# Chunk 0's joins by 64-row products of block-diagonal operands, and sums of squares ahead of the second pair of turned keys, in a delta-rule attention with a feed-forward behind it

## The chip, the cores and the metric

The kernel runs on one core of one Trainium2 chip. The metric is the device time in microseconds; less is better. A run of the unchanged kernel gives a median of 650.97 us over three (650.86 to 651.51). Besides that there is one profiled execution, from which all durations are taken.

## The reference

Four batches and eight heads of 768 tokens with 48 features go through a delta-rule recurrence; the result, as 3072 rows of 384, goes through a feed-forward with SiLU.

```python
    k_n = k / (np.linalg.norm(k, axis=-1, keepdims=True) + 1e-06)
    for t in range(S):
        kt, vt, bt = (k_n[:, :, t], v[:, :, t], beta[:, :, t, None])
        y[:, :, t] = np.einsum('bhd,bhde->bhe', q[:, :, t], state)
        v_old = np.einsum('bhde,bhd->bhe', state, kt)
        state = state + bt[:, :, :, None] * np.einsum('bhd,bhe->bhde', kt, vt - v_old)
...
    h = x @ w_in
    g = h * (1.0 / (1.0 + np.exp(-h)))
    return (g @ w_out).astype(np.float32)
```

`w_in` is 384 x 2048, `w_out` 2048 x 384, everything in 32-bit floats.

## The kernel before

**Tiling.** The sequence is cut into six chunks of 128 tokens, a chunk into two halves (`hf`) of 64, a half into two blocks of T = 32. The four batches form two groups `g` of two; a group has 16 heads (HH). A chunk's recurrence becomes a triangular system in the scores of the keys with each other. Its diagonal 32x32 blocks are inverted for all heads at once, with the (block, head) pairs on the 128 partitions, on VectorE (`invert_first` for chunk 0, `invert` for the others); TensorE then joins the inverted blocks to 64x64 inverses (`xi`), by which the values are multiplied (`inner`, L830). Chunk 0 is made in two halves, so that its feed-forward can start early: `joins(0)` runs before anything of the feed-forward, `joins(1)` in pieces between its products.

**Chunk 0's inversion and joins.** `invert_first` inverts only the 16x16 corners of each 32x32 block (`x`), for both corners at a time: one multiplication by `step` (L658), 15 pairs of L666 and L670, one last multiplication (L673). Q = 16 is the size of a corner. Two transposes bring the result from pairs on partitions to tokens on partitions: `low` (L680, the first 16 rows of each block) and `up` (L684, all of it). POOL copies the second half of the identity into `y` (L681). Then come the stages that `joins` (L1364) lists:

- `corner(g, hf)`: the scores of a 32-row block, transposed, by `low`: one product of 32x32 by 32x16 for each of two blocks of 16 heads (L707). Two operations on VectorE (L714, 64 rows each) multiply by the mask `second`, add the identity `pick`, and write `y`.
- `turned(g, hf)`: `up` by `y` for the even block of each head (L723), copied out to `xes` by ScalarE and VectorE.
- `straight(g, hf)`: `y` by `up` for both blocks, two products of 32x32 by 32x32 for each head (L736), copied out in four pieces to the diagonal blocks of `xi`.
- `merge_half(g, hf, second)`: two stages of 16 products of 32x32 (L796) for the off-diagonal block.

All is in 32-bit floats, for which each product stands twice in TensorE's program: 16 products are 32 pairs of a weight load (PEld) and a matmul (PE) in the profile. So a `corner` or `straight` is 64 pairs, a `turned` or a `merge_half` 32, and one `joins` 128 + 64 + 128 + 128 = 448.

`joins` takes a list `between`, one entry behind each stage: `sizes_0` finishes the key lengths on VectorE (L420, L423), `sized` multiplies half of the values by them on POOL (`size_half`, L447, which waits for the operation of VectorE named last), and `filled(n)` and `begin_next` run steps of `narrow`.

**Front.** Keys of chunk 0 are loaded in four batches by six transfers; POOL squares them (`square`, L375), TensorE transposes them (`turn`, L490), VectorE or ScalarE copies them out (L502, L504), TensorE makes the key-by-key blocks (`first_blocks`, L1274), VectorE sums the squares (`add_squares`, L379) and computes the reciprocal lengths with three Newton steps (`norm_steps`, L393 to L413). `beta_of` (L351, L354) brings the gates to tokens on partitions. `block_steps` (L435, L440) makes `step`; `blocks_in` is the VectorE transpose of the blocks. `busy(n)` (L338) issues n products of 128x128 by 128x384 that nobody reads (two passes each).

**Weights.** `w_in` comes in eight pieces of 768 KB (`fetch_w_in(i)`), `w_out` likewise. `narrow` rewrites a piece by two operations on ScalarE (L226, L227), two on VectorE (L231, L235) and one on POOL (L239), the steps of which are spread by `fill`, `begin_next` and their like.

**What sets the order.** `pin` keeps every engine's instructions in the order of the program text; nothing is reordered. Loads go out from SP in one line (`in_line`). `linked(fetch, ...)` lets the next transfer wait until the one before it in line has landed. While chunk 0's inversion runs, a list of words per step places `first_score` ("s", L519), `turn` of the queries ("u"), `score` with the queries ("w") and `busy` ("b", behind the named step). After `joins(0)` one long text (`script`) orders what follows by hand: "s" a step of chunk 0's solve (`inner`, `first_outputs`, ...), "f" a step of `narrow`, "j5" five pairs of `joins(1)`, "r" a piece of the feed-forward (`hidden`, L1031), "T" and "q" transposes of chunk 1, "W7" `fetch_w_in(7)`.

## Time and profile before

| | |
|---|---|
| time, median of three | 650.97 us |
| profiled execution: its time, its span | 653.34 us, 651.36 us |
| granted TensorE clock, mean | 0.976 |

Busy time in stretches of 10 us:

| us | PE | DVE | ACT | POOL | PE clock | GB/s |
|---|---|---|---|---|---|---|
| 10 to 20 | 6.48 | 8.73 | 1.78 | 3.35 | 0.75 | 196 |
| 20 to 30 | 9.68 | 8.97 | 8.52 | 1.94 | 0.74 | 163 |
| 30 to 40 | 5.29 | 7.01 | 2.95 | 6.90 | 0.60 | 151 |
| 40 to 50 | 6.16 | 3.91 | 4.96 | 1.82 | 0.50 | 170 |
| 50 to 60 | 10.00 | 5.08 | 5.60 | 1.85 | 0.87 | 167 |
| 60 to 70 | 9.85 | 8.04 | 8.24 | 3.75 | 1.00 | 132 |
| 70 to 80 | 9.62 | 8.76 | 7.05 | 8.39 | 1.00 | 182 |

PE, DVE, ACT, POOL and SP are TensorE, VectorE, ScalarE, GpSimd and the engine that issues the loads. "PE clock" is the share of full speed that was granted. In rows of the timeline, "x21" is a count, and "[2.84 <-issue]" says that the engine had been idle for 2.84 us and that no other engine or transfer is seen to have released it. The first product of the feed-forward (L1031) starts at 56.55 us.

### The profile page before, as it was taken

How to read it: one execution, taken by the hardware profiler on the slowest of the kernel's cores; microseconds unless marked ns; L12 is line 12 of the kernel's file. 1: busy time of each engine (PE TensorE's matmuls, PEld its weight loads, DVE VectorE, ACT ScalarE, POOL GpSimd, SP SyncE). 2: the span in 40 equal slices, each digit the busy share in tenths (PEclk: the TensorE clock that was granted, in tenths of full speed). 3: DMA queues.
4: the chain of work that ended last, by engine and by line, in shares of the span. 5: the costliest groups of instructions: out<-in, count | busy, mean ns of one | idle time of the engine just before them, and what ended most of it. 6: DMA issues, size and time to landing. Idle time of an engine off the chain costs nothing.

```text
span 651.4 us, 21809 instructions
## 1 busy us (share of the span) xinstructions
PE 627.3 (96%) x9644; PEld 550.7 (85%) x9644; DVE 394.3 (61%) x902; ACT 216.3 (33%) x505; POOL 95.7 (15%) x96
## 2 busy tenths in 40 slices
PE   6859999999999999999999999999999999899997
PEld 4648778666789988989989989989989989789997
DVE  5955979988764985554975453986455963103112
ACT  1646666251351122451122451122451122351111
POOL 5231730337011020010020010020011000000000
PEclk9758999999999999999999999999999999999999
DMA  9675444160369433269243259334163023100101
GB/s 171 141 185 149 148 123 105 49 146 3 78 129 155 60 77 46 60 131 159 43 94 34 57 126 151 59 77 50 41 140 71 24 68 43 40 13 1 25 0 25
DMA packets 141310, 53.68 MB, mean 82 GB/s; under 512 B 112912, under 2 KB 134672, under 8 KB 141216
## 3 DMA queue, kind: packets, MB, share of 16 engines
q1 hardware_dynamic: 140880, 52.14, 40.1%
q8 instruction: 76, 1.25, 0.8%
q10 hardware_dynamic: 336, 0.15, 0.1%
q14 instruction: 18, 0.15, 0.1%
HBM read 39.62 MB, written 10.49 MB: 77 GB/s over the span
## 4 chain that ended last, share of the span: by engine, by line
PE 85%; DVE 8%; DMA 2%; issue 2%; ACT 1%; SPq 1%; POOL 0%; DVEq 0%; POOLq 0%
PE phid L1031 35%; PE px L1138 15%; PE py L1138 11%; PE po L1066 7%; PE pa L519 3%; PE pz L830 3%; DVE rank L617 2%; PE pu L850 2%; PE ph L818 2%; DVE x L622 2%; PE pyc L909 2%; PE pt L490 1%; PE pyc L896 1%; PE px L772 1%; PE py L772 1%
## 5 line engine op out<-in xcount | busy, mean ns | idle before, releaser
L1031 PE MATMUL phid<-xT,w_in 128*128 128x256 f32 x1152 | 258.4, 382 | 2.0 <-DMA xT<-part 2.0
L1031 PEld LDWEIGHTS phid<-xT,w_in 128*128 128x128 f32 x1152 | 215.9, 190 | 33.4 <-issue 3.5
L1041 ACT ACTIVATE gT<-phid 128x512 f32<-128x512 f32 x88 | 52.6, 598 | 143.6 <-PE phid L1031 140.8
L617 DVE SCALAR_TENSOR_TENSOR rank<-g,step,x 128x31 f32<-128x31 f32 (+15 forms) x124 | 49.8, 401 | 35.6 <-DMA g<-blocks 32.2
L1120 DVE TENSOR_TENSOR sums_of_g<-gT 128x384 f32<-128x384 f32 (+1 forms) x60 | 30.1, 521 | 58.9 <-ACT gT L1041 48.3
L1138 PE MATMUL px<-sums_of_w,sums_of_g 128*128 128x192 f32 x320 | 56.8, 329 | 0.0
L1138 PE MATMUL py<-w_out,sums_of_g 128*128 128x192 f32 x320 | 56.8, 329 | 0.0
L1138 PEld LDWEIGHTS px<-sums_of_w,sums_of_g 128*128 128x128 f32 x320 | 52.2, 190 | 0.5
L1138 PEld LDWEIGHTS py<-w_out,sums_of_g 128*128 128x128 f32 x320 | 52.2, 190 | 0.4
L622 DVE TENSOR_TENSOR x<-x,rank 128x31 f32<-128x31 f32 (+15 forms) x124 | 42.5, 342 | 4.3
L457 POOL TENSOR_TENSOR vf<-vf,n_slot 128x768 f32<-128x768 f32 x10 | 15.3, 1539 | 174.5 <-DMA vf<-in_v_dram 123.4
L478 DVE STREAM_TRANSPOSE kq<-stage 128x512 f32<-128x512 f32 x28 | 28.6, 1114 | 8.1 <-DMA stage<-in_q_dram 7.6
L534 ACT COPY xT<-pyc 48x128 f32<-48x128 f32 (+2 forms) x126 | 32.6, 259 | 1.6
L1138 PE MATMUL px<-sums_of_w,gT 128*128 128x192 f32 x160 | 28.4, 329 | 0.0
L1138 PE MATMUL py<-w_out,gT 128*128 128x192 f32 x160 | 28.4, 329 | 0.0
L1138 PE MATMUL px<-w_out,gT 128*128 128x192 f32 x160 | 28.0, 327 | 0.0
L830 PEld LDWEIGHTS pz<-vf,xi 64*64 64x64 f32 x768 | 25.2, 142 | 3.2 <-issue 2.9
L540 POOL COPY g<-x 64x256 f32<-64x256 f32 x4 | 5.0, 1240 | 151.9 <-DVE x L625 151.9
L1138 PEld LDWEIGHTS px<-w_out,gT 128*128 128x128 f32 x160 | 26.4, 190 | 0.5
L830 PE MATMUL pz<-vf,xi 64*64 64x48 f32 x768 | 26.9, 226 | 0.0
L1138 PEld LDWEIGHTS py<-w_out,gT 128*128 128x128 f32 x160 | 26.1, 190 | 0.3
L1138 PEld LDWEIGHTS px<-sums_of_w,gT 128*128 128x128 f32 x160 | 26.1, 190 | 0.2
(197 smaller groups left out, 833.8 us busy)
## 6 DMA issues: line engine op xcount, KB each, us to landing
vf<-in_v_dram SPq DMA_DIRECT2D x48, 96.0 KB, 3.3
out_dram<-o SPq DMA_DIRECT2D x42, 96.0 KB, 2.2
w_out<-in_moe_w_in_dram SPq DMA_DIRECT2D x4, 768.0 KB, 6.0
sums_of_w<-in_moe_w_out_dram SPq DMA_DIRECT2D x4, 768.0 KB, 4.9
blocks<-ap SPq DMA_DIRECT2D x40, 64.0 KB, 1.9
g<-blocks SPq DMA_DIRECT2D x5, 512.0 KB, 3.7
kb<-in_k_dram SPq DMA_DIRECT2D x12, 192.0 KB, 4.6
kb<-in_k_dram SPq DMA_DIRECT2D x24, 96.0 KB, 4.5
```

The lines of the kernel that those rows point to most:

```text
L457: pin(nc.gpsimd.tensor_tensor(out=vf, in0=vf, in1=of, op=ALU.mult))
L478: pin(nc.vector.transpose(out=kqs[c, b][:, :, j, :].rearrange("p a (i m) -> p a m i", i=T), in_=src.rearrange("p a (m d) -> p a m d", d=D) ...
L519: pin(nc.tensor.matmul(pa[e][half, p * n * W : (p + 1) * n * W], lhsT=kq[rows, p, 0, half], rhs=kq[rows, p, js[0] : js[-1] + 1, half], sta ...
L534: return pin(nc.scalar.copy(to, of))
L617: pin(nc.vector.scalar_tensor_tensor(out=tv, in0=g[:, 0:m, m : m + 1].to_broadcast([P, m, n]), scalar=step[:, m : m + 1], in1=x[:, m : m + ...
L622: yield pin(nc.vector.tensor_tensor(out=x[:, 0:m, m:T], in0=x[:, 0:m, m:T], in1=tv, op=ALU.add))
L830: yield pin(nc.tensor.matmul(pz[rows, n * D : (n + 1) * D], lhsT=xis[g][rows, u * H + 2 * p + e, :], rhs=vfs[c][rows, hf, g * HB + u, p, : ...
L1031: pin(nc.tensor.matmul(ph[:, j * GT : (j + 1) * GT], lhsT=w_in[:, a, (2 * f + j) * P : (2 * f + j + 1) * P], rhs=xTs[c, hf][:, a, :], star ...
L1041: pin(nc.scalar.activation(out=hidden_of(c, hf, f), in_=ph[:], func=ACTF.Silu, scale=-0.5 if in_blocks(c) else 0.5))
L1066: pin(nc.tensor.matmul(pos[i][:, 0:DM], lhsT=hidden_of(0, hf, f // 2)[:, at : at + C], rhs=w_outs[f // HFF][:, f % HFF, :], start=(f == 0) ...
L1120: pin(nc.vector.tensor_tensor(out=sums_of_g[:, k, fs], in0=of[0], in1=of[1], op=op))
L1138: pin(nc.tensor.matmul(to, lhsT=at, rhs=quarter(f, *b) if isinstance(b, tuple) else sums_of_w[b][:, f], start=start and f == 0, stop=f == ...
```

## The change

Operands become block-diagonal, so that the two 32-row products of a head are one of 64 rows.

- `y` is replaced by `wides`: 64x64 for each head, with both blocks on the diagonal and zeros beside them, in three places (a work tile, part of `sum_room`, `crossed`). They are filled from `pick_w`, a constant that POOL makes at the start, by three copies on ScalarE; POOL's copy L681 is gone.
- `low` becomes `lows`, 32 columns for a head: two halves of 16, the second zero for the even block (two POOL memsets behind the inversion), and a copy of the first for the odd one (one copy of 32 rows on ScalarE, one on VectorE, between the two transposes). In the odd blocks the first half holds the same values.
- The lower left 32x32 squares of the key scores are set to zero on POOL (four memsets, behind `first_score`).
- `corner` and `straight` issue 16 products in place of 32. `corner` is followed by four L714 operations of 32 rows in place of two of 64.
- `add_squares` moves ahead of the second pair of `turn`s, whose copies both go to ScalarE; `beta_of(0)` moves between the last two `first_blocks`; `busy(1)` becomes `busy(3)`.
- `load_k(1)` goes ahead of `fetch_w_in(0)`; `load_v(0)` waits for `fetch_w_in(1)`; pieces 5 and 6 of `w_in` change places.
- The words within the inversion, the list `between` and the long text are rewritten.

```diff
+    pick_w = const.tile([P, W], FP32, name="pick_w")
+    pin(nc.gpsimd.memset(pick_w[:], 0.0))
+    for j in range(NB):
+        rows, cols = slice(T * j, T * (j + 1)), slice(T * (j % 2), T * (j % 2 + 1))
+        pin(nc.gpsimd.tensor_copy(out=pick_w[rows, cols], in_=ident[rows, rows]))
...
+    wides = {}
+    def wide_of(n):
+        return wides[n // HH, n % 2][:, n % HH // 2]
...
-        low = sum_room[:, AT_LOW : AT_LOW + BH * Q].rearrange("p (n s) -> p n s", s=Q)
-        y = sum_room[:, AT_G : AT_G + BH * T].rearrange("p (n s) -> p n s", s=T)
...
-        pin(nc.vector.transpose(out=low.rearrange("p n s -> p s n"), in_=x[:, 0:Q, :]))
-        pin(nc.gpsimd.tensor_copy(
-            out=y[:, :, Q:T], in_=pick[:, Q:T].unsqueeze(1).to_broadcast([P, BH, Q])
-        ))
+        lows = sum_room[:, AT_G : AT_G + BH * T].rearrange("p (n i s) -> p n i s", i=2, s=Q)
+        for j in (0, 2):
+            pin(nc.gpsimd.memset(lows[rows[j], :, 1], 0.0))
+        pin(nc.vector.transpose(out=lows[:, :, 0].rearrange("p n s -> p s n"), in_=x[:, 0:Q, :]))
+        for k, by in enumerate((by_act, by_dve)):
+            by(lows[rows[2 * k + 1], :, 1], lows[rows[2 * k + 1], :, 0])
...
-                for j in (2 * k, 2 * k + 1):
-                    cols = slice(T * (j % 2), T * (j % 2 + 1))
-                    pin(nc.tensor.matmul(
-                        pls[k][rows[j], Q * i : Q * (i + 1)], lhsT=aps[0, g][0][rows[j], n % HH // H, n % H, cols],
-                        rhs=low[rows[j], n, :], start=True, stop=True,
+                half = HALVES[k]
+                pin(nc.tensor.matmul(
+                    pls[k][half, T * i : T * (i + 1)], lhsT=aps[0, g][0][half, n % HH // H, n % H, :],
+                    rhs=lows[half, n].rearrange("p i s -> p (i s)"), start=True, stop=True,
+                ))
+                yield
+            for k in range(2):
+                for odd in range(2):
+                    of, at = rows[2 * k + odd], T * odd
+                    pin(nc.vector.scalar_tensor_tensor(
+                        out=wides[g, hf ^ k ^ g][of, :, at : at + Q],
+                        in0=out_of(pls[k], of, T)[:, :, Q * odd : Q * (odd + 1)], scalar=second[of],
+                        in1=pick[of, 0:Q].unsqueeze(1).to_broadcast([T, HH // 2, Q]), op0=ALU.mult, op1=ALU.add,
                     ))
...
-                for j in (2 * k + 1, 2 * k):
-                    pin(nc.tensor.matmul(
-                        pls[k][rows[j], T * i : T * (i + 1)], lhsT=y[rows[j], n, :],
-                        rhs=up[rows[j], n, :], start=True, stop=True,
-                    ))
-                    yield
+                half = HALVES[k]
+                pin(nc.tensor.matmul(
+                    pls[k][half, T * i : T * (i + 1)], lhsT=wide_of(n)[half],
+                    rhs=up[half, n, :], start=True, stop=True,
+                ))
+                yield
...
+    for b in range(B):
+        add_squares(0, b)
     for b in range(2):
         first_blocks(b)
     for b in range(2, B):
-        turn(0, b, 0, (A, CC)[b % 2], b % 2 == 0)
-    for b in range(2, B):
-        first_blocks(b)
-    for b in range(B):
-        add_squares(0, b)
+        turn(0, b, 0, (A, CC)[b % 2], False)
+    first_blocks(2)
     beta_of(0)
-    busy(1)
+    first_blocks(3)
+    busy(3)
     for t in xis:
         pin(nc.gpsimd.memset(t, 0.0))
+    wide_x = work.tile([P, HH, W], FP32, name="wide", tag="x", bufs=1)[:]
+    low_w = sum_room[:, AT_LOW : AT_LOW + BH * T // 2].rearrange("p (n s) -> p n s", s=W)
+    cross_w = crossed[:].rearrange("p n s -> p (n s)").rearrange("p (n s) -> p n s", s=W)
+    for to in (wide_x, low_w, cross_w):
+        pin(nc.scalar.copy(out=to, in_=pick_w[:].unsqueeze(1).to_broadcast([P, to.shape[1], W])))
...
+    load_k(1)
     fetch_w_in(0)
-    load_k(1)
     fetch_w_in(1)
-    load_v(0)
+    linked(load_v, 0)
...
+    for j in (1, 3):
+        pin(nc.gpsimd.memset(aps[0, 0][0][T * j : T * (j + 1), :, :, 0:T], 0.0))
     busy(1)
...
+    linked(fetch_w_in, 5)
     linked(fetch_w_in, 6)
-    linked(fetch_w_in, 5)
...
-        for word in ["s2 u0", "u1", "w0", "s3 u2", "w1", "u3", "", "w2 w3", "", "", "", "", "", "", "", "", "", "", "", "", "", ""][n].split():
+        for word in ["s2 u0 u1 w0", "", "", "u2 s3", "", "", "w1 u3", "w2", "", "w3", "", "", "", "", "b", "", "", "", "", "", "", ""][n].split():
...
-    together(joins(0, [none, none, sizes_0, sized, filled(2), none, none, begin_next, filled(1), none]))
+    together(joins(0, [none, sizes_0, none, sized, none, filled(2), begin_next, none, none, filled(1)]))
```

The long text began "s f2 s T f T q s q T j5 j16 j8 f j5 f r q T j20 j5 b r" and now begins "s2 f T T s q f q T j5 f j16 j8 f r j5 f b q T j4 j20 r"; later words of it move by a few places.

More of the change, by code (lines that the diff above doesn't have):

```diff
@@ L704, in corner @@
             for i, n, k in heads(g, hf):
-                for j in (2 * k, 2 * k + 1):
-                    cols = slice(T * (j % 2), T * (j % 2 + 1))
-                    pin(nc.tensor.matmul(
-                        pls[k][rows[j], Q * i : Q * (i + 1)], lhsT=aps[0, g][0][rows[j], n % HH // H, n % H, cols],
-                        rhs=low[rows[j], n, :], start=True, stop=True,
-                    ))
-                    yield
-            for k in range(2):
-                of = slice(W * k, W * (k + 1))
-                pin(nc.vector.scalar_tensor_tensor(
-                    out=of_half(y[of], g, hf, k)[:, :, 0:Q], in0=out_of(pls[k], of, Q), scalar=second[of],
-                    in1=pick[of, 0:Q].unsqueeze(1).to_broadcast([W, HH // 2, Q]), op0=ALU.mult, op1=ALU.add,
-                ))
+                half = HALVES[k]
[11 more added lines that the diff above has]
+                        in1=pick[of, 0:Q].unsqueeze(1).to_broadcast([T, HH // 2, Q]), op0=ALU.mult, op1=ALU.add,
+                    ))
         def turned(g, hf):
@@ L724, in turned @@
                     pls[k][rows[2 * k], T * i : T * (i + 1)], lhsT=up[rows[2 * k], n, :],
-                    rhs=y[rows[2 * k], n, :], start=True, stop=True,
+                    rhs=wide_of(n)[rows[2 * k], 0:T], start=True, stop=True,
                 ))
@@ L1343 @@
         done = next(inv)
-        for word in ["s2 u0", "u1", "w0", "s3 u2", "w1", "u3", "", "w2 w3", "", "", "", "", "", "", "", "", "", "", "", "", "", ""][n].split():
+        for word in ["s2 u0 u1 w0", "", "", "u2 s3", "", "", "w1 u3", "w2", "", "w3", "", "", "", "", "b", "", "", "", "", "", "", ""][n].split():
             at = int(word[1:] or 0)
-            if word[0] == "b":
+            if word[0] == "s" and at % HB == 1:
+                first_score(at)
+                for j in (1, 3):
+                    pin(nc.gpsimd.memset(aps[0, at // HB][0][T * j : T * (j + 1), :, :, 0:T], 0.0))
+            elif word[0] == "b":
                 busy(1, done, Sync)
```

5 lines of the change are left out of this document (2 added, 3 removed).

## The prediction

> **What bounds the kernel now.** I read the clock line and the fetch line of the page, then the chain that ended last, then the timeline of all engines up to 60 us.
>
> ```profile
> PE 627.3 (96%) x9644; PEld 550.7 (85%) x9644; DVE 394.3 (61%) x902; ACT 216.3 (33%) x505; POOL 95.7 (15%) x96
> ...
> PEclk9758999999999999999999999999999999999999
> ...
> q8 instruction: 76, 1.25, 0.8%
> ```
>
> From about 50 us TensorE never stops for long, so what is won ahead of that point is won at the end, and what is won later counts only as TensorE work. From 8 to 48 us TensorE is not the bound, and its clock is at half from 32 to 52 us (0.60 and 0.50 in the windows of 30 to 50). The third line gives the unit of what follows: 19,288 loads and products in 76 packets are 254 a packet, so TensorE's program comes in pieces of 256 instructions, or 128 pairs of a load and a product.
>
> The chain, in order of time (start, length, what):
>
> ```profile
> 15.95 0.36 DVE nr L409
> ...
> 17.56 0.60 PE pg L435 x2
> ...
> 18.80 0.70 DVE sums_of_w L658
> ...
> 29.27 1.05 DVE sums_of_w L680
> 30.32 1.77 DVE sums_of_w L684
> ...
> 34.05 2.84 issue
> ...
> 39.36 2.08 issue
> ...
> 44.32 2.38 issue
> 46.69 0.95 PE px L796 x26
> 47.64 3.48 PE pz L830 x62
> ```
>
> VectorE sets it up to 32.1 us: lengths of the keys, then the inversion (18.80 to 29.2), then two transposes. Then come chunk 0's joins, and in them TensorE stands still three times "for nothing that the profile shows", 7.30 us in all. The timeline tells what these gaps are (start, busy, what, count, idle before):
>
> ```profile
> 14.24 0.69 PE L1274 MATMUL blocks<-kq 48*32 48x32 f32 x56 [2.30 <-issue]
> 15.04 1.65 PE L338 MATMUL pw<-state,ident 128*128 128x384 f32 x2
> ...
> 36.89 0.74 PE L723 MATMUL pl<-sums_of_w 32*32 32x32 f32 x21 [2.84 <-issue]
> ...
> 41.44 0.92 PE L736 MATMUL pl<-sums_of_w 32*32 32x32 f32 x53 [2.08 <-issue]
> ...
> 46.69 0.95 PE L796 MATMUL px<-xi,xe_y 32*32 32x32 f32 x26 [2.38 <-issue]
> ```
>
> Adding the counts of all rows between the restarts at 36.89 and 41.44 gives 26 of L723, 70 of L736 and 32 of L796: 128 pairs. From 41.44 to 46.69 it is 58 + 32 + 38 = 128 again. So TensorE stops at each end of a 256-instruction piece. A piece is asked for when an earlier one is used up: restarts lie 4.55 and 5.25 us apart, and the border before, 128 pairs ahead of the gap at 34.05 (38 pairs into L707, 30.8 us), lies 6.1 us before its restart. The joins therefore cost about 5.3 us for each 128 pairs, however short the products are.
>
> [...]
>
> **The change, part by part.**
>
> Front (to L658). The four sums of squares no longer stand behind the copy of the third pair of keys. The squares are ready at 7.95 and 10.55 us on POOL, a sum takes 0.48, so the lengths start at 11.1 in place of 12.93 and L413 ends at 15.6 in place of 17.41: 1.8 us won on VectorE. beta_of(0) moves ahead of the last key blocks, and so ahead of the gap that ends at 14.24, so it is in time. But block_steps' product (L435) stands on TensorE behind busy(3), six passes in place of two. They start at 15.0, when the blocks are done. The two took 1.65 at half clock, and the first ones of the kernel start 0.64 apart (3.20, 3.84, 4.48): 6 x 0.64 = 3.84, and L435 starts at 18.9 where it started at 17.56. The copy of step ends 0.85 later (18.39 - 17.56 in before), so L658 starts at 19.75, 0.95 late. At full clock a pass of 384 columns takes 0.327 (L1066, 20.26 for 62): six are 2.0, L435 starts at 17.0, blocks_in is done by then (15.6 + 1.25), L658 starts at 17.6, 1.2 early. The clock fell at 15.0 in this execution, and the passes themselves may bring it back before the last: I take +0.5, ends -1.2 and +0.95.
>
> [...]
>
> Three copies of the picked identity on ScalarE (128x1024 and two of 128x512; 0.58 for 128x512, L504) are 2.3 us between 12.4 and 14.7, where it waits (it sat idle 2.85 us before the copy of step, 3.76 before beta_tok): nothing. POOL's five small operations for pick_w take 1.1 us (0.94 for L327's four) in its 2.06 us of waiting for keys: nothing. Clearing the off-diagonal squares of the scores is four memsets on POOL, 0.52 each at most (L307), in the 14.65 us that it waits before L681. The pass "b" ends by 29.5, before the corners. Without that cover each would cost its length.
>
> SP: six issues of k(1) now stand ahead of w_in(0), whose last packet was done at 16.3. k(0) took 5.25 us to issue, so w_in(0) goes out at 15.3 and lands about 20 (a tensor of this size takes 5.2 to 6); ScalarE takes it up at 21.61. v waits for w_in(1) (last packet at 23.0, still so), lands near 29.5 and is used at 38. Behind it on SP stand w_in(2) and q(1): each linked fetch moves by some 1 us, but they landed 8 us and more before their narrowing (third fetch: issued 45, narrowed 59.55). Nothing, with rival C.
>
> Joins of hf 0 (before: L658 to first L830 = 47.57 - 18.80 = 28.77). The corners fall from 128 pairs to 64, the straights from 128 to 64, the rest stays: 448 pairs become 320, one piece less. With 6 pairs more ahead (two more busy products and "b", two passes each), the borders lie 32, 160 and 288 pairs in: in the middle of the corners, at the first merge, at the last merge. *Bound by pieces*: low is ready 12.15 us after L658 (29.27 + 1.05, and a copy of 32x512, 0.6, on ScalarE and VectorE as in the later copies to crossed and xi); first border at 14.0, then 4.55 twice, then the last merge 0.85: first L830 at 24.0, so -4.8. *Bound by the chain*: a pass of 64x64 is not in the joins of before; the nearest is L830 at half clock, two at a time: 3.48/62 = 56 ns. Corners 2 x 32 x 56 = 3.6, to 15.8. VectorE: up's transpose to 14.0, then eight L714 in place of four at 0.36 (fewer rows do not shorten one): to 15.5 and 17.3. Turned(1) behind that, 1.1: 18.4. The sizes (1.7 in before, most of it one 1.13 copy beside POOL) and two copies on VectorE: 19.85. Straight(0) 1.8, merge 0.85, straight(1) 1.8, merge 0.85: 23.7. ScalarE begins the third w_in (1.9) ahead of that merge's copy: 25.85; last merge: 26.7, so -2.1. The two lie 2.7 apart. Larger tiles may open the clock sooner, and the ScalarE work filled gaps before; I take the middle, -3.3.
>
> Joins of hf 1 lie in full TensorE at full clock, and gaps count nothing there. Before: L707 0.72 for 58 pairs (12.4 ns) and L736 0.62 for 46 (13.5): 128 of each are 3.3 us, four tiles at a time. After, 128 pairs of 64x64, two at a time: 28 ns if the clock halves L830's 56, so 3.6; 16.9 ns if as fast as L850's 1.08 for 64, so 2.2; the nearer row is L830: +0.3, ends -1.1 and (56 ns) +3.9. The four L714 more (1.44) lie beside phid passes. The order written by hand moves steps and leaves their count: nothing.
>
> Sum: +0.5 - 3.3 + 0.3 = -2.5 on the span of 651.36, which is 648.9; the profiled execution's 653.34 has 1.98 around it and is 2.4 over the median. Against the median: 650.97 - 2.5 = **648.5 us**, own range 646.5 to 650.2.
>
> **Rivals.**
>
> B, more than forecast: the six passes meet full clock, or the joins do: front -1.2, joins -4.5, second joins 0: 645.3. For it: 1.8 us are free on VectorE. Against: the half clock at 15.0.
>
> C, no change: w_in(0) lands with the later of the two tensors, at 23.0. ScalarE then stands at L226 for 1.4 us, with the scores' copies and now also low's copy behind it, and with step 0.5 later low is ready 1.9 us late: -2.5 + 1.9 = -0.6, 650.4. Against: 192-byte packets of k need 4 to 5 us, not 8.
>
> D, slower: the 64-row pass costs 56 ns at full clock too, bound by loading 64 columns and not by the clock. Then the hf 1 joins cost +3.9, the hf 0 joins give the chain's -2.1 and the front +0.5: +2.3, 653.3. It turns slower from 38 ns a pass (1.6 us over 128). For: nowhere above do two such tiles run alone at full clock. Against: L850's 16.9.
>
> E, the change doesn't save what it says: the gaps are not fetches and stay. Then low's copy 0.6, two more L714 on the path 0.7, front 0.5, hf 1 joins 0.3: +2.1, 653.1. Against: 128 and 128 pairs.
>
> **How the numbers follow.** No change means within 0.2%, 1.3 us, about what a measurement here can tell. Forecast 0.52, B 0.17, C 0.14, D 0.11, E 0.06. Faster: B, and the forecast but for 0.03 of its upper end: 0.66. Within: C and these 0.03: 0.17. Slower: D and E, 0.17. The range 645.0 to 652.3 leaves out D and E, and a little below B: 0.19.
>
> **What would show it.** Right: two gaps or fewer in the hf 0 joins, 128 pairs apart, and the first L830 at 43.5 to 46. Front: L658 at 19.3 if the six passes hold it, 17.6 if not. Second joins: 64 corner passes in 1.8 us at full clock; 3.6 would be D. C would show as a wait of L226 for DMA. The forecast is wrong if three gaps remain, or if the first phid product comes earlier than 56.55 and the end does not.

## The result and the profile after

The changed kernel takes 656.13 us (median of 9 runs, 653.51 to 662.83); the kernel before, run beside it, 651.18 (9 runs, 649.87 to 652.84). The ratio is 1.0086, 95% interval 1.0062 to 1.0109: slower, where 648.5 was forecast, and outside the range of 645.0 to 652.3. The profiled execution took 658.49 us, with a span of 656.8 and a mean granted clock of 0.973 (before 653.34, 651.4, 0.976).

From the page of the changed kernel, its busy times, its clock line and its fetch line:

```profile
PE 637.9 (97%) x9394; PEld 559.3 (85%) x9394; DVE 394.9 (60%) x910; ACT 219.0 (33%) x510; POOL 98.8 (15%) x106
...
PEclk9759998999999999999999999999999999999999
...
q8 instruction: 74, 1.21, 0.8%
```

There are 250 products fewer (256 of the joins and 6 more idle passes) and two packets of the instruction queue fewer, as the change says; and yet TensorE is busy 10.6 us longer. Of this, 5.3 us lie between 20 and 50 us (26.47 busy against 21.13): the gaps of the joins have turned into slow products at half clock (0.50 granted from 30 to 50 us), not into an earlier end.

The chain that ended last, in order of time (start, length, what), shows where the start went:

```profile
16.02 5.11 DMA raw<-in_moe_w_in_dram
21.18 0.80 issue
21.98 0.96 ACT raw L227
24.02 1.13 PE pa L524 x32
...
31.07 1.58 PE pw L343 x2
32.65 3.65 PE pl L716 x63
37.53 1.06 PE pl L734 x32
38.59 1.85 PE pl L747 x32
...
46.23 1.05 PE px L807 x30
47.28 3.48 PE pz L841 x62
```

Before, the same stretch began with VectorE (the inversion, the transposes) and had three "issue" entries of 7.30 us in it. Now the longest such entry there is 0.80, on ScalarE, and the chain runs through the load of w_in(0) and ScalarE's narrowing of it. Rows of the timeline show how that reaches the joins (start, busy, what, count, idle before and its releaser):

```profile
17.68 0.69 DVE L668 TENSOR_TENSOR sums_of_w<-sums_of_w,step 128x512 f32<-128x512 f32 x1 [1.38 <-ACT step L445]
...
21.15 0.92 ACT L226 ACTIVATE w_in<-raw 128x768 f32<-128x768 f32 x1 [0.98 <-DMA raw<-in_moe_w_in_dram]
21.98 0.96 ACT L227 ACTIVATE raw<-raw,plus 128x768 int32<-128x768 uint32 x1
...
24.02 1.13 PE L524 MATMUL pa<-kq 48*64 48x64 f32 x32 [2.13 <-ACT kq L505]
...
26.12 1.99 PE L524 MATMUL pa<-kq 48*64 48x64 f32 x64
...
27.86 1.06 DVE L691 STREAM_TRANSPOSE sums_of_w<-sums_of_w 128x512 f32<-128x512 f32 x1
...
31.12 0.65 ACT L539 COPY ap<-pa 128x256 f32<-128x256 f32 x2 [0.21 <-PE pa L524]
31.79 0.62 ACT L539 COPY sums_of_w<-sums_of_w 32x512 f32<-32x512 f32 x1
32.58 3.69 PE L716 MATMUL pl<-sums_of_w,ap 64*64 64x32 f32 x64
```

The first multiplication of the inversion (L668, before L658) starts 1.12 us earlier than before. VectorE has `low` at 28.92. Its copy for the odd blocks stands on ScalarE behind the copies of the scores, and these behind L226, which waited for the load. TensorE, too, stands still for 2.13 us ahead of 24.02, its granted clock is at half from 23.9 on (0.50 from 24 to 32), and the scores and their copies come late for that as well. So the copy ends at 32.41, and the corners start at 32.58, where they started at 30.47.

Much later there is a second wait that the kernel before did not have. TensorE, about 100 us into the span:

```profile
96.99 0.30 PE L440 MATMUL pg<-pick,spread 128*128 128x32 f32 x2
97.13 1.54 PE L1042 MATMUL phid<-xT,w_in 128*128 128x256 f32 x6
98.77 1.16 PE L524 MATMUL pa<-stage 48*64 48x64 f32 x64
101.32 0.69 PE L524 MATMUL pa<-stage 48*64 48x64 f32 x32 [1.39 <-ACT step L445]
```

And ScalarE in the same stretch:

```profile
98.74 0.94 ACT L226 ACTIVATE w_out<-w_out 128x768 f32<-128x768 f32 x1
99.57 0.99 ACT L227 ACTIVATE w_out<-w_out,plus 128x768 int32<-128x768 uint32 x1
100.59 0.60 ACT L1052 ACTIVATE gT<-phid 128x512 f32<-128x512 f32 x1
101.08 0.18 ACT L445 COPY step<-pg 128x32 f32<-128x32 f32 x1
```

The new long text puts three products of scores behind the word "g" (block_steps of chunk 1) where the old one put two. The third needs the bank out of which ScalarE copies `step`, and ScalarE has two operations of narrowing and an activation to do first.

Against the profile before, the first phid product (L1042, before L1031) comes 0.60 us later, the 78th 1.87, the 96th 3.88, the 111th 4.88, the last 5.42. The profiled time is 5.15 longer, so nearly the whole loss between these two profiles lies ahead of 110 us.

### The profile page after: what moved, and what is told of

The parts are those of the page before. It is cut to its first block, busy times and chain, and to the rows that moved or that the text cites. A ratio compares the mean times of both kernels' runs of the same rounds, so it can differ in the third digit from the quotient of the medians.

```text
span 656.8 us, 21333 instructions
## 1 busy us (share of the span) xinstructions
PE 637.9 (97%) x9394; PEld 559.3 (85%) x9394; DVE 394.9 (60%) x910; ACT 219.0 (33%) x510; POOL 98.8 (15%) x106
## 4 chain that ended last, share of the span: by engine, by line
PE 80%; DVE 5%; SPq 5%; DMA 4%; ACT 3%; issue 2%; POOL 1%; POOLq 0%; DVEq 0%; ACTq 0%
PE phid L1042 31%; PE px L1149 14%; PE py L1149 11%; PE po L1077 6%; PE pa L524 3%; PE pz L841 3%; DVE rank L622 2%; DVE x L627 2%; PE pu L861 2%; SPq L142 2%; PE pyc L920 2%; PE ph L829 2%; PE pt L495 1%; PE pyc L907 1%; SPq L900 1%
## 5 line engine op out<-in xcount | busy, mean ns | idle before, releaser
L1042 PE MATMUL phid<-xT,w_in 128*128 128x256 f32 x1152 | 260.1, 384 | 2.0 <-DMA xT<-part 2.0
L1042 PEld LDWEIGHTS phid<-xT,w_in 128*128 128x128 f32 x1152 | 217.1, 191 | 33.8 <-issue 3.4
L841 PEld LDWEIGHTS pz<-vf,xi 64*64 64x64 f32 x768 | 25.0, 142 | 3.2 <-issue 2.9
L841 PE MATMUL pz<-vf,xi 64*64 64x48 f32 x768 | 26.6, 226 | 0.0
```

Of the source, the lines that this page charges most:

```text
L841: yield pin(nc.tensor.matmul(pz[rows, n * D : (n + 1) * D], lhsT=xis[g][rows, u * H + 2 * p + e, :], rhs=vfs[c][rows, hf, g * HB + u, p, : ...
L1042: pin(nc.tensor.matmul(ph[:, j * GT : (j + 1) * GT], lhsT=w_in[:, a, (2 * f + j) * P : (2 * f + j + 1) * P], rhs=xTs[c, hf][:, a, :], star ...
```

## The experiments

All ratios are to runs of the kernel before made beside them on the same chip, with 95% intervals.

**Undoing parts of the change.**

x1, products of 32 rows in both halves, from the same block-diagonal operands:

```diff
-                pin(nc.tensor.matmul(pls[k][half, T * i : T * (i + 1)], lhsT=aps[0, g][0][half, ...],
-                    rhs=lows[half, n]...))
+                for odd in range(2):
+                    pin(nc.tensor.matmul(pls[k][of, ...], lhsT=aps[0, g][0][of, ...], rhs=lows[of, n, 0], ...))
```

> The changed kernel with corner and straight issuing two 32-row products for a head again, in both halves, from the same operands (lows and wides); all else is the change's. Theory that the 64-row products cost more than the pieces of program they save: the hf 1 joins win back 0.9 us (64 passes of 32.2 ns for corners and 32.8 for straights become 128 of 12.4 and 13.5), and 0 to 2 us are won in the hf 0 joins, so about 654 to 655 us against the change's 656.1. Theory that a 256-instruction piece costs 5 us wherever the joins run ahead of the feed-forward: one more gap of 2 to 3 us, 128 pairs from the next, appears in the hf 0 joins, the first L841 comes 1 to 2 us later than the change's 47.2, and the time is 656 to 658. Theory that the gaps are not fetches: no new gap and the first L841 near 44.

Measured: 657.83, ratio 1.0109 (1.0071 to 1.0147). Stops for "nothing that the profile shows" are back, of 0.71 and 1.91 us in the first joins, 128 pairs apart, and of 1.57 in the second. The products of 64 rows are not what makes the change slow as a whole. The `inner` products start at 44.15, 3.1 us ahead of the change's, where the theory whose time fits had them 1 to 2 us later; the median shows nothing of that gain. Rows of x1:

```profile
21.70 0.90 ACT L226 ACTIVATE w_in<-raw 128x768 f32<-128x768 f32 x1 [1.41 <-DMA raw<-in_moe_w_in_dram]
...
25.75 1.16 PE L524 MATMUL pa<-kq 48*64 48x64 f32 x64
...
29.72 1.44 PE L717 MATMUL pl<-sums_of_w,ap 32*32 32x16 f32 x128
```

x1 has the change's order of loads. ScalarE waits longer for w_in(0) than in the change (1.41 against 0.98), and yet the corners start 11.92 us after the first multiplication, where the change needs 14.90. What differs is TensorE's pace: 64 products of scores take 1.16 us here and 1.99 there (at 26.12), at a granted clock of 0.50 from 24 to 32 us.

x2, the word "g" five words later in the long text:

```diff
-... l p l3 f r g r f p v b p2 i ...
+... l p l3 f r r f p v b g p2 i ...
```

> The change with one word of the long text moved: the product for chunk 1's step comes behind the first of the remaining score pairs, as it did before the change, so that only two scores stand between it and the use of its bank. Theory that the order of the text costs: the wait of a score for the copy of step near 100 us (1.4 to 1.6 us in the change's profile) and the half clock behind it go, and the time falls by 1.5 to 3, to 653 to 654.6. Theory that the loss is in the products and the front: that wait goes, and the time stays within 0.7 of the change's 656.1, with the order of feed-forward pieces catching up elsewhere.

Measured: 654.10 (10 runs), 1.0050 (1.0022 to 1.0078). The wait for L445 is gone. TensorE near 100 us in x2:

```profile
99.60 0.69 PE L524 MATMUL pa<-stage 48*64 48x64 f32 x32
100.29 0.41 PE L440 MATMUL pg<-pick,spread 128*128 128x32 f32 x2
100.63 1.16 PE L524 MATMUL pa<-stage 48*64 48x64 f32 x64
```

All three products of scores run without a stop around L440. The medians differ by 0.36%, a size that the two intervals cannot pin down alone.

x3, w_in(0) loaded ahead of chunk 1's keys again:

```diff
-    load_k(1)
     fetch_w_in(0)
+    load_k(1)
```

> The change with the first piece of w_in fetched ahead of chunk 1's keys, as it was before the change; the rest of the loads stay in the change's order. Theory that the late weights hold ScalarE: L226 no longer waits (it started at 21.15 with the landing), no gap of 2.4 us on TensorE near 22, the scores end 1.5 to 2.5 us earlier, the first corner comes at 30 to 31 in place of 32.6 and the first L841 at 45 to 46 in place of 47.2; the time falls by 1 to 2, to 654 to 655. Theory that the corners are held by the extra pass and the 64-row products alone: the first L841 within 0.7 of 47.2, the time unchanged.

Measured: 655.78, 1.0065 (1.0044 to 1.0086). The corners start 12.04 us after the first multiplication, where the change needed 14.90, and the first product of `inner` (L841) comes at 45.59 in place of 47.21, although that multiplication was 1.68 later. In x3 64 products of scores take 1.16 us (at 25.88), as in x1. The end hardly shows the gain.

x4, without the idle pass "b":

```diff
-... "w3", "", "", "", "", "b", "", ...
+... "w3", "", "", "", "", "", "", ...
```

> The change without the one product that waits for the inversion's 14th step (the word b), which ran from 31.00 to 32.65 just ahead of the first corner. Theory that this product holds the corners: the first corner comes 1 us or more earlier (31.1 to 31.6), and the first L841 with it. Theory that ScalarE's copy of low (31.79 to 32.41 in the change, behind the late scores) holds them anyway: the first corner at 32.4 to 32.6, and nothing is won; the time within 0.7 of 656.1.

Measured: 656.37, 1.0081 (1.0052 to 1.0110); corners at 33.01. The pass that stands ahead of the corners in the chain holds nothing: ScalarE's copy does, late as in the change, with 1.99 us for 64 products of scores here too (at 26.63).

**Which part.** y1 is the change with the old long text (each product of 64 rows yields twice, so that the counts of "j" fit), y3 the same with x3's order of loads; y2 is the kernel before with the new long text alone (two products of 32 rows count as one step), y4 the kernel before with the new front alone.

```diff
-        "s2 f T T s q f q T j5 f j16 j8 f r j5 f b q T j4 j20 r j8 ...
+        "s f2 s T f T q s q T j5 j16 j8 f j5 f r q T j20 j5 b r j8 ...
```

> The change with the long text of before: its 64-row products, front, loads, words within the inversion and list between stay, and each 64-row corner or straight product counts as two steps, so that the old text's numbers fit. Theory that the rewritten text costs: the wait of a score for the copy of step near 100 us (1.6) and the one of 1.6 between transposes near 186 go, and between the first and the 78th pass of the feed-forward the loss against before falls from 1.3 us to the 0.9 that the 64-row passes of hf 1 cost; time 652.5 to 653.5 against 656.1. Theory that products and front cost, and the text only hides or shows it: the time stays within 0.8 of 656.1, the waits move elsewhere.

> The kernel before with the new long text alone; a 32-row corner or straight pair counts as one step, so that the new text's numbers fit. Theory that the rewritten text costs by itself: the score waits 1.3 to 1.6 us for the copy of step, a wait of about 1.6 appears between the transposes behind it, and pieces of 256 instructions run dry in the hf 1 joins, which the text leaves with fewer feed-forward passes between; time 653.5 to 655.5 against 651.2. Theory that the text is neutral and the products cost: 650.5 to 652.

> The change with the long text of before and with the first piece of w_in fetched ahead of chunk 1's keys: both edits together. Theory that late weights and the text make up the loss, each by itself: first L841 1.6 us ahead of the change's 47.2, no wait for step, time 650.5 to 652, no longer slower than before. Theory that the 64-row products are the loss: 654 or more.

> The kernel before with the front of the change alone: sums of squares early, the second pair of keys copied by ScalarE, beta_of(0) earlier, three unread products in place of one. Theory that the front is a gain: the first inversion product at 17.6 to 17.8 in place of 18.80, the first L830 about 1 us ahead of 47.57, time 649.5 to 650.5. Theory that the piece fetches decide when the joins end, whatever the front does: the first L830 within 0.5 of 47.57 and the time within 0.6 of 651.2.

Measured: y1 655.59, 1.0083 (1.0051 to 1.0114); y2 657.15, 1.0108 (1.0072 to 1.0145); y3 654.44, 1.0059 (1.0035 to 1.0083); y4 651.13, 1.0008 (0.9985 to 1.0032). The new text makes the old products slower by 1.08%, and its profile has the wait for L445 (1.59 us). But the old text does not make the new products faster by the medians (y1), although y1's profile, its fastest run, has no such wait. What y1 keeps is a stop near 183 us, which the change has as well (1.62 us from product to product, ahead of 187.83). Rows of y1:

```profile
181.89 0.33 PE L922 MATMUL pyc<-ap,z 64*64 64x64 f32 x5 [0.81 <-issue]
182.15 1.09 PE L495 MATMUL pt<-ident,kb 128*128 128x128 f32 x8
184.56 1.09 PE L495 MATMUL pt<-ident,kb 128*128 128x128 f32 x8 [1.31 <-ACT xT L539]
```

From product to product it is 1.58 in y1, between the two rows of transposes, and 1.03 before it, at a border of the program among the last products of L922. The kernel before has 0.66 between its transposes and 1.07 at a border. The change loses nothing by its stop: from the 111th to the 289th phid product it takes 120.10 us, as the kernel before does. y1 takes 121.74, of which 1.11 are lost here. So y1 has lost the wait for L445 and gained a loss of 1.6 later, and the rest of its median stays unexplained by its profile.

The front (y4) alone shows no gain in the median. In its profile the first multiplication starts at 19.41, 0.61 later than before, since a stop of TensorE in `first_blocks` (11.94 to 14.67) was followed by unread passes 0.64 apart. Over all profiles the first multiplication starts at 18.1 on the mean of ten with the new front and at 18.5 of eight with the old.

**One part alone.** z1 is the kernel before with the block-diagonal operands and products alone, old text and loads; z2 with the order of loads alone; z3 is z1 with 32-row products in the second half; z0 is the kernel before unchanged, for one more profile.

```diff
+                    if hf == 1:
+                        pin(nc.tensor.matmul(pls[k][of, ...], ..., rhs=lows[of, n, 0], ...))
+                    elif odd == 0:
+                        pin(nc.tensor.matmul(pls[k][half, ...], ..., rhs=lows[half, n]..., ...))
```

> The kernel before, unchanged, for a second profile: its profiled execution (653.34) lay 2.2 above the median of its runs. Theory that the profile of before is a slow execution: this one lies at 650 to 652, and its stages show where the 2 us are, in the half clock of the first 55 us (20.5 us of it in the joins) or in the last 400 us (from the 289th feed-forward pass to the last 406.05 in before, 404.4 to 405 in most others). Theory that it is a typical one: all stages within 0.5 us of the first profile.

> The kernel before with the block-diagonal products alone (their operands, clearing and copies included); front, loads, words, list and long text are those of before. Theory that the 64-row products cost more than the piece of program they save: first L841-like product (inner) no earlier than 1 us ahead of before's 47.57 because corners and straights take 57 ns a pass at half clock, the hf 1 joins 1 to 2 us longer (0.9 of it passes), time 652 to 655. Theory that the products are a gain and the order around them loses it: the inner product at 44 to 45, time 648.5 to 650.5.

> The kernel before with the load order of the change alone (chunk 1's keys ahead of the first piece of w_in, the values behind the second piece's landing, pieces 5 and 6 exchanged). Theory that late weights hold ScalarE: it waits 1 us or more for the first piece near 20 us, TensorE stands at the scores, the clock stays low longer, the inner product comes 0.5 to 2 us later, time 651.5 to 653. Theory that the piece fetches hide it: inner product within 0.5 of 47.57, time within 0.6 of before.

> The kernel before with the block-diagonal products in the hf 0 joins alone; the hf 1 joins issue 32-row products from the same operands, and the rest is before's. Theory that the hf 1 joins lose and the hf 0 joins win: inner product 2 to 3 us ahead of 47.57 as in the products alone, the feed-forward's first 78 passes as long as before, time 648 to 650. Theory that the hf 0 products win nothing either: inner product within 1 us of 47.57, time 651 to 653.

Measured: z0 657.24 in its one run (clock 0.971); z1 652.93, 1.0031 (1.0012 to 1.0051); z2 651.67, 1.0003 (0.9981 to 1.0024); z3 652.23, 1.0026 (1.0003 to 1.0049). The restarts of TensorE in z0, on the timeline:

```profile
35.58 0.75 PE L723 MATMUL pl<-sums_of_w 32*32 32x32 f32 x21 [1.72 <-issue]
39.03 0.92 PE L736 MATMUL pl<-sums_of_w 32*32 32x32 f32 x53 [0.98 <-issue]
42.91 0.95 PE L796 MATMUL px<-xi,xe_y 32*32 32x32 f32 x26 [1.00 <-issue]
...
69.60 0.22 PE L796 MATMUL py<-xe_y,ap 32*32 32x32 f32 x2 [0.72 <-issue]
73.05 0.46 PE L850 MATMUL pu<-z,kb 64*64 64x48 f32 x5 [0.90 <-issue]
```

The same program, the same three borders, the same counts (x21, x53, x26), and 3.70 us of stops where the first profile had 7.30. Its `inner` began 3.78 earlier. Yet two new stops follow at later borders, and the 78th phid product is 0.35 later than in the first profile. z2 does the same: 4.09 earlier at the first phid, 1.00 later at the 78th. Neither theory of z0 held: it was not faster than the first profile, and its stages differ by up to 3.8 us. In z1 and z3 the `inner` products start 2.2 and 2.4 us ahead of 47.57, near to what the theory of a gain had, and the times are those of the other theory.

z1 shows what the second joins cost. The waits of TensorE between 50 and 95 us in z1 (total, times, longest):

```profile
PE pl L735 <- DVE crossed L725: 0.5, 1, 0.5
PE pa L524 <- issue: 0.5, 1, 0.5
PE px L809 <- ACT xe_y L539: 0.3, 1, 0.3
PE pl L735 <- DVE sums_of_w L725: 0.3, 1, 0.3
```

From the first to the 78th phid product z1 loses 1.96 us against the first profile of the kernel before; z3, with 32-row products there, 0.52. That distance is itself a draw for 32-row products: it is 33.4 in before, 33.1 in y4 and p1, but 36.8 in z0 and 38.5 in z2. With 64-row products and the old text it is 35.3 in all four profiles (y1, y3, z1, c2), without a stop for "nothing that the profile shows" in the joins. Rows of z1: 64 corner passes take 2.3 us between their neighbours (34, 26 and 4 of them, 1.17 + 0.93 + 0.24) where 128 pairs took 1.6, which is 0.7; `turned` waits 0.8 for the four scalings of VectorE; 64 straight passes cost some 0.4 more. That sums to 1.9, though z3 has the waits of `turned` too (0.9) and still loses only 0.52. By the medians z1 and z3 cannot be told apart.

**The price of a piece.** p1 is the kernel before with each product of the first joins' corners issued twice, into the same place: 128 pairs more, one piece.

```diff
+                    for _ in range(2 - hf):
                         pin(nc.tensor.matmul(pls[k][rows[j], ...], ..., rhs=low[rows[j], n, :], ...))
```

> The kernel before with each corner product of the hf 0 joins issued twice (same place, same values), 128 pairs of load and product more, which is one piece of 256 instructions; they take 1.3 us of TensorE, of which 0.6 is hidden by the transpose of up. Theory of the prediction, that each piece costs a round trip of 4.5 to 6 us there: four gaps in the profile, inner product and time 4.5 to 6 us later, 1.007 to 1.009. Theory that in ordinary executions the fetch keeps up better than in the first profile (gaps of 4.4 in all in the second): time 2 to 3.5 us later, 1.003 to 1.0055. Theory that gaps are not fetches: 0.5 to 1 us later.

Measured: 655.87, 1.0063 (1.0038 to 1.0088), so 4.1 us. Its restarts:

```profile
36.42 1.49 PE L708 MATMUL pl<-sums_of_w,ap 32*32 32x16 f32 x88 [4.05 <-issue]
40.77 0.74 PE L724 MATMUL pl<-sums_of_w 32*32 32x32 f32 x21 [1.57 <-issue]
45.59 0.92 PE L737 MATMUL pl<-sums_of_w 32*32 32x32 f32 x53 [2.35 <-issue]
50.30 0.95 PE L797 MATMUL px<-xi,xe_y 32*32 32x32 f32 x26 [1.83 <-issue]
```

One stop more, each 128 pairs after the last, and 4.35, 4.82 and 4.71 us from restart to restart. The prediction took 5.3 for a piece: right in kind. The 4.1 lie between the ranges of the first two theories, and the interval reaches into both, so p1 cannot tell them apart; only the third, that the gaps are not fetches, is out.

**Mending the change.** c1 is the change with x2's text and x3's loads; c2 is z1 with the copy of `low` on POOL in place of ScalarE; c3 is the change with all three.

```diff
-        for k, by in enumerate((by_act, by_dve)):
+        for k, by in enumerate((by_pool, by_dve)):
```

> The change with both single edits that won something: the word for chunk 1's step behind the first of the remaining scores, and the first piece of w_in ahead of chunk 1's keys. Theory that the loss of 0.86% is the sum of products (0.31), step (0.36) and late weights (0.2): what is left is the products, 1.002 to 1.004 times before. Theory that the two edits mend the same wait, or that the rest of the rewritten text costs too: 1.005 or more.

> The block-diagonal products alone on the kernel before, with the copy of low for the first half's odd block on POOL in place of ScalarE, where it stood behind the scores' copies (31.14 to 31.76) while the first corner waited from 30.20 to 31.85. Theory that ScalarE's queue holds the corners: the first corner at 30.6 to 31.0, the inner product 0.8 to 1.2 us earlier, 1.001 to 1.002 times before. Theory that the 57 ns passes and the four L714 set the joins: the inner product within 0.4 of where it was relative to the first corner's cause, 1.003 as without the edit.

> The change with the step's word, the weights first and the POOL copy of low together. Theory that the three and nothing else cost: 0.999 to 1.002 times before, at best no different from it. Theory that 64-row passes at half the array's parallel tiles cost by themselves: 1.003 or more.

Measured: c1 653.12, 1.0043 (1.0020 to 1.0066); c2 651.96, 1.0020 (1.0002 to 1.0039); c3 652.73, 1.0031 (1.0013 to 1.0049). c1 lies between its two theories. For c3 the median is that of the theory that the 64-row passes cost by themselves, though the interval reaches into the other. Half of the loss or more is mended and the rest stays. No version is faster than the kernel before.

## Why the prediction was wrong

The first joins are best seen from three times of each profile: the first multiplication of the inversion, the first corner, the first product of `inner`. In us, with the distances from the first of them worked out:

| profile | first multiplication | corner | inner | to corner | to inner |
|---|---|---|---|---|---|
| before | 18.80 | 30.47 | 47.57 | 11.67 | 28.77 |
| z0, before again | 18.59 | 30.29 | 43.79 | 11.70 | 25.20 |
| z2, 32 rows | 18.58 | 30.44 | 43.67 | 11.86 | 25.09 |
| y2, 32 rows | 18.70 | 30.40 | 46.12 | 11.70 | 27.42 |
| y4, 32 rows | 19.41 | 31.09 | 46.61 | 11.68 | 27.20 |
| the change | 17.68 | 32.58 | 47.21 | 14.90 | 29.53 |
| x2, keys first | 17.52 | 32.86 | 47.50 | 15.34 | 29.98 |
| y1, keys first | 17.65 | 29.72 | 44.59 | 12.07 | 26.94 |
| x3, weights first | 19.36 | 31.40 | 45.59 | 12.04 | 26.23 |
| c1, weights first | 18.55 | 30.60 | 44.83 | 12.05 | 26.28 |
| z1, products alone | 18.41 | 31.85 | 45.33 | 13.44 | 26.92 |
| c2, copy on POOL | 17.69 | 30.11 | 43.67 | 12.42 | 25.98 |

**"Joins of hf 0 (before: L658 to first L830 = 47.57 - 18.80 = 28.77)": the step that failed first, by its base.** Both halves of its working were near. The pieces: with 128 pairs fewer no stop falls on a border in the first joins of z1, c2 or z3, the one in the change (ahead of 46.23) is released by a copy of ScalarE's, and with 128 more there is one more. (ScalarE narrows the third w_in ahead of that copy, as forecast. In z1, c2 and z3 TensorE last stops for 1.2 us just ahead of `inner`, and in z1 that ends when the copies of `xi` are through, which stand behind steps of `narrow` until 44.72 on VectorE and 44.85 on ScalarE.) But the price of a piece was not fixed: in z0 the restarts lie 3.45 and 3.88 apart, where 5.3 was taken. The chain: the first L830 at 26.7 after the first multiplication was forecast for *bound by the chain*, and where the copy of `low` is not held the runs have 26.0 to 26.9. But 28.77 was one draw. The five profiles of the first joins as they were before the change give 25.1 to 28.8, mean 26.7: the very figure of the chain, which is luck. So -3.3 is 0 on the mean: the pieces go, and a chain of VectorE, ScalarE and half-clock passes of the same length is left. The rate of the passes was foreseen (56 ns, measured 3.65/63 = 58 in the change). This would also join p1 to z1: one piece more costs 4.1 us, one piece less wins nothing, for below the old length the chain takes over; that is argued from these profiles, not tested by itself. In the change `inner` starts at 47.21, outside the 43.5 to 46 that would have shown the forecast right. Taking the middle between the two bounds added to the error. That larger tiles open the clock sooner, a part of that choice, no run shows: with 64-row products the change is at half clock from 23.90 to 51.21, as before is from 32.08 to 52.56. And that a piece is asked for when an earlier one is used up was the author's reading of 4.55, 5.25 and 6.1 us; when it is asked for, no view shows.

**"Nothing, with rival C" (the loads), and "low is ready 12.15 us after L658".** Where 64 products of scores take 1.16 us, 12.04 to 12.07 was measured in x3, c1 and y1, and 11.92 in x1. In the profiles of the change, x2 and x4 it was 14.9 to 15.5: L226 waited for w_in(0), the scores' copies stood behind it, and the copy of `low` behind those. That is C's queue, but its price is the clock. All five profiles with the change's front and loads have the wait of L226 (0.98 in the change, 1.45 in x2, 1.64 in x4, 0.78 in y1, 1.41 in x1). In the first three 64 products of scores take 1.99 us, in the change at the half clock that begins at 23.90, and the delay is 2.9 to 3.4; in y1 and x1 they take 1.16, and there is none. C's 1.9 was worked out from the wait alone. x3 mends it in the profile, and by 0.2% in the median, which the intervals don't establish. In z1, with the old loads, the same copy waits 1.4 us for four copies of scores alone; POOL's copy in c2 removes that.

**"The order written by hand moves steps and leaves their count: nothing" was wrong.** The row at 101.32 has a stop of 1.4 us that the text makes, and in this profile the clock is at half behind it (102.41 to 105.82), together 3.0 us from the 78th phid to the 111th. In x1, x3, x4 and y2, with the same wait, that stretch is only 1.3 longer than in before; the 1.7 between is half of the 3.41 us at half clock. y2 shows that the text costs by itself, 1.08%; x2 shows that the word "g" is the place of that wait. The text alone doesn't decide the sign: y1 without it is still slower. Moving a step past another means moving it ahead of or behind a bank's release too, and the prediction counted instructions only.

**The second joins** were put at +0.3 with 28 ns a pass. Measured were 1.87/58 = 32 for the corners and 1.05/32 = 33 for the straights, four 32-row tiles at 12.4 and 13.5 before: 64 x 32.2 + 64 x 32.8 - 3.3 = +0.9. And the "four L714 more" do not lie beside phid passes in z1: `turned` waits 0.8 for them. Rival D (56 ns at full clock) is out. The right mechanism, mis-sized by 0.6 us in the passes, and by up to 1.6 with the wait. That "gaps count nothing there" failed in z0 and z2, where the distance from the first to the 78th phid product is 3.4 and 5.1 us longer, with stops of up to 1.0 us for "nothing that the profile shows" and, in z0, a granted clock of 0.83 from 70 to 80 us.

**The step "what is won ahead of that point is won at the end"** failed with it: what z0 and z2 had won by the first phid product (3.06 and 4.09) was gone by the 78th, and z1 and z3 are, by their medians, no faster for the 2.2 and 2.4 us that their `inner` products come earlier. With 64-row products and the new text it held as far as the 78th: the distance is 34.6 to 34.7 in six profiles whose first phid product lies anywhere between 54.6 and 59.0.

**The front** was put at +0.5, bounds -1.2 and +0.95. The change drew -1.1, x3 +0.6, y4 +0.6. Both ends occur, but not for the reason forecast. In the change the six passes run at half clock (0.52 from 13.5 to 17) and take 3.7 us, as in x3; they start at 13.38 in place of 15.0, since TensorE's stop in `first_blocks` was 1.02 us where the first profile has 2.30 and x3 2.31. So in these profiles the length of that stop decides, and full clock for most of the passes, which the early end took, was not seen. That the passes bring the clock back before the last was the author's estimate: in the change it came back at 17.07, just ahead of L440 at 17.12.

**Rival E** (no fetches) is out by p1 and by the stops that vanished. **B** had the early front, for the same other reason, and joins 4.5 shorter, which no run gave.

By the medians, the products alone cost 0.31%, the word "g" some 0.36%, the late weights some 0.2%: 0.87 of the 0.86 measured. That the sum fits is luck: each part has an interval of about 0.2 to 0.35 either way, and the parts don't add, since the new text costs 1.08% on the old products (y2) and taking it out of the change wins 0.03 (y1). What is established without such sums: the products alone are slower, c1 is slower than the kernel before, and the change with all three mended still is. Why y1's median keeps the full loss is open: its one profile is its best run, and the 1.6 us that it loses late are a part of it at most. Open too is where z1 loses its 0.31%: its profile is 1.96 longer in the second joins than the first profile of the kernel before but shorter than z0 and z2 there, and z3's median does not separate from it.

## What to carry to other kernels

A stall that the profile shows once is a draw (7.30 us of stops in one execution here, 3.70 in the next): look at a second execution of the same kernel before putting its length into a sum, and ask what the next bound is when it is gone, as here the chain behind the fetches was just as long. A copy added to an engine waits for everything that is queued ahead of it there (1.4 us of score copies in z1), a wait for a load among it (0.98 us in the change), and the half clock behind stops of TensorE can cost more than the stops: near 565 us they are 0.39 us longer in z0 than in the first profile of before, and z0 loses 3.7 us. When an order written by hand is changed, follow for each moved step which buffer it frees and who copies out of it, not only how many instructions there are.

## What the runs showed of the hardware

The stops in the first joins, 128 pairs apart, come at the same instructions in both profiles of the kernel before (the rows behind them count 21, 53 and 26) but differ in length: 7.30 us in the first and 3.70 in the second. And time won by shorter stops was given back within 40 us in z0 and z2, by stops at later borders (0.91 and 1.11 us from product to product in z0, 1.19 and 1.12 in z2) and, in z0, by a granted clock of 0.83 from 70 to 80 us. From restart to restart the first joins take 3.45 to 5.25 us in z0, p1 and the first profile, and p1 puts the price of one piece at 4.1 us. What TensorE waits for at these stops no view shows by itself; that it is the next piece of the program rests on the 128 pairs between them, on p1, and on the instruction queue: 76 packets for 19,288 loads and products before, 74 for 18,788 in the change, 254 a packet.

In the change a fp32 product of 64 by 64 rows, on two places in turn, takes 58 ns a pass at half clock and 32 to 33 at full, where 32-row products, on four places in turn, take 12.4 and 13.5 each at full clock before (L707, L736): two of these are cheaper than one of 64 rows, so that in this case the larger tile could pay only where instructions are the limit.

Stops of much the same length were followed by half clock in some places and not in others. In the profiles of the kernel before and of the change the granted clock changes only at whole multiples of 3.41 us from its other changes (in before at 15.01, 25.25, 32.08 and 52.56 us, in the change at 13.66, 17.07, 23.90, 51.21, 102.41 and 105.82). Taken in stretches of 3.41 us between such points, it fell after stretches at full clock in which TensorE stood still for 2.30 and 1.09 us in all in before (up to 15.01 and 32.08) and for 1.27, 2.01 and 1.38 in the change (up to 13.66, 23.90 and 102.41); it held after others with 1.34 in before (up to 567.97) and 1.25 in the change (up to 187.74). A length from which it falls is not shown. Near 565 us the kernel before has three stops in which TensorE waits for the transfers of its last rows: 0.70, 0.52 and 0.82 us in the first profile of the kernel before, 1.08, 0.53 and 0.82 in z0, the same kernel. In z0 the first two lie in one such stretch, in which TensorE works 1.39 us of 3.41; in the first profile the first lies ahead of a border at 564.56, and TensorE works 2.07. In z0 the clock is at 0.79 and 0.53 in the two stretches of 5 us from 565 on, where the first profile has 1.00 in both, and its end falls back by 3.7 us against its place at the 289th phid product. Two windows of z0 and one of the first profile:

```profile
565.00:570.00 5.00, 3.08 (x30) 0.79 0.33 80
570.00:575.00 5.00, 5.00 (x121) 0.53 0.14 33
```

```profile
565.00:570.00 5.00, 3.65 (x134) 1.00 0.43 103
```

The columns are the stretch, its length, TensorE's busy time and products, the granted clock, and the transfers' share and rate. So one execution of an unchanged kernel lost 3.7 us here, where the medians of the change and of the kernel before differ by 4.95.
